# Attention scores by one full float32 product instead of three products of rounded halves, in a fused attention and feed-forward kernel

## Chip, cores and metric

The kernel runs on one core of a Trainium2 chip. The metric is device time in microseconds of one launch, as the median of several runs. Before the change it is 913.26 us, the median of three runs from 912.97 to 914.45 us.

## What is computed

Attention over 8 batches of 8 heads, with keys and values averaged over blocks of 8 tokens, followed by a feed-forward layer. Queries and keys are drawn 8 times larger than normal, so that the scores have to be accurate.

```python
# q, k, v: (8, 8, 576, 64) float32
k_p = k.reshape(B, H, 72, 8, D).mean(axis=3)
v_p = v.reshape(B, H, 72, 8, D).mean(axis=3)
scores = scale * np.matmul(q, k_p.transpose(0, 1, 3, 2))
scores = scores - np.max(scores, axis=-1, keepdims=True)
attn = np.exp(scores)
attn = attn / (np.sum(attn, axis=-1, keepdims=True) + 1e-09)
x = np.matmul(attn, v_p)        # to (4608 tokens, 512)
h = x @ w_in                    # 512 -> 2048
g = h * erf(softplus(h))
out = g @ w_out                 # 2048 -> 512
```

The scores alone are what the change touches.

## The kernel before

**Numbers in halves.** The products use the type `float32r`, into which values are rounded. What must be accurate is made of three such products: high half by high half, high by low, low by high. The high half is a rounded copy of a value (a cast on ACT, sometimes DVE or POOL), the low half is the difference (a subtraction on DVE or POOL).

**Chunks.** The 4608 tokens are worked off in nine chunks of 512. The first two chunks use plain products for the first layer (`gemm1`, L817). From the third on, a scheme with seven half-size products in place of eight does it (`products`, L762). The second layer (`gemm2`, L866) is the same for all.

**Attention.** `job` (L510) handles one block of up to 320 tokens of one batch. Keys of a new batch are summed over 8 tokens into `ks` and stored, as high and low halves, in `kbd`, a block-diagonal array: for each of the four pairs of heads, 144 columns of high halves and 144 of low ones, with the two heads of a pair on partitions 0 to 63 and 64 to 127. `softmax_tile` then takes up to 128 queries. There are 40 such tiles: 32 with 128 queries and 8 with 64. A tile's queries come by DMA into `raw`; ACT makes `qh` (L346, a helper for all copies; some go to DVE or POOL at L349 and L347), POOL or DVE makes `ql` (L584).

**Scores before.** In the first two chunks, and for tiles of 64 queries throughout, PE makes three products for each pair of heads (L618), 144 columns each: 12 a tile, in two groups of two pairs. DVE takes the maximum of a group from PSUM (L623) and, outside the first chunk, subtracts it (L640). In the first chunk ACT takes the exponential straight from PSUM with the maximum as its bias (L634). From the third chunk on a tile of 128 queries is scored in another form (25 tiles, `wide_scores`). For each pair of heads, the high half of the queries goes over all 288 columns of `kbd` (L594), and the low half over 144 (L596), which is two weight loads and two products in place of three and three. This form leaves two partial sums side by side, so ACT copies one out (L600), DVE adds the other (L602), takes the maximum of all eight heads (L605) and subtracts it (L607).

After that the tile's softmax (L649 to L666) is the same in both forms. PE transposes the result (L673, L680), and four products with the values for each pair of heads follow (L714).

**Order.** No engine's order is written by hand. The program is recorded as operations with an engine, a guessed cost and a due time, and `Program.order` lays them out greedily by these guesses; each engine then executes its own list strictly in order. Buffers have fixed numbers of copies: `raw` 2, `qh` and `ql` 1 each, PSUM 8 banks with caps by use. The first chunk borrows the space of late weights for a second `qh` and `ql` (`LENT_Q`). While PE has nothing to do in the first 57 us of the planner's time, the planner puts dummy products into its list (L929, 202 of them). DMA is issued by SP, in the same planned order.

Of the kernel before, what the change touches and what calls it, by code (L numbers as in the profile page):

```python
# [11 lines left out]
F32 = mybir.dt.float32  # L12
# [39 lines left out]
ON_ACT = ((1, 1), (1, 1), (1, 1), (1, 1))  # L52

LENT_E = ("wo15", "wo14", "wo13")
LENT_Q = ("wi15", "wo12")
LENT_KV = ("wo8", "wo9", "wo10", "wo11", "wi9", "wi10", "wi11", "wi12", "wi13", "wi14")
WIDE_FROM = 2
SLACK, BIAS = 34, 1150
FILL, MARGIN = 57000.0, 300
DGE = 2000  # L60
# [244 lines left out]
def moe_attention(ctx: ExitStack, tc: tile.TileContext, cst, qa, kl, vl, wi, wo, out):  # L305
# [3 lines left out]
    if wide:  # L309
# [2 lines left out]
    ctx.enter_context(tc.manual_schedule(engines={E.PE, E.Activation, E.DVE, E.Pool, E.SP}))  # L312

    const = pool("const", 1)
    sizes = {"t": 8, "raw": 2, "qh": 1, "ql": 1, "eth": 1, "etl": 1, "etb": 1,
             "s": 2, "m": 2, "z": 2, "bb": 1, "ks": 1, "vs": 1, "hs": 3, "y": 1, "f": 2, "gh": 3, "gl": 2}
    pools = {t: pool(t, n) for t, n in sizes.items()}
    banks = pool("banks", 8, space=PSUM)
# [14 lines left out]
    def dve(n):  # L333
        return 1.04 * n + 95
# [38 lines left out]
    def late(tag, shape, dtype=F32):  # L373
        return Buf(weights, [P] + shape, dtype, tag, [tag])

    kbd = const.tile([P, NP, 4 * SP], F32R, name="kbd")
    vah = const.tile([P, NP, P], F32R, name="vah")
    val = const.tile([P, NP, P], F32R, name="val")
    vb = const.tile([P, NP, D], F32R, name="vb")
    nc.gpsimd.memset(kbd.bitcast(F32), 0.0)  # L380
    KBD, VA, VB = (Kept() for _ in range(3))
    def f32(ap):
        return ap.bitcast(F32)
# [126 lines left out]
    def job(ck, b, tiles, off, times, first, fresh):  # L510

        base, due = times[0], times[-1] + VAL_R
        if fresh:
            ks, vs = buf("ks", [NP, SP]), buf("vs", [NP + 2, D])

            on_dve = b < ON_DVE

            def load_pool(src, dst, p, size, prio, tag):
                t = (loan if tag in LENT_KV else buf)(tag, [size, POOL] if on_dve else [POOL, size])
                op("SP", (14.4 if first and p < NP and size == SP else 10.3) * size, prio - 1, lambda: nc.sync.dma_start(  # L520
                    t.ap, src.rearrange("(p a b) -> p a b", p=P, b=t.ap.shape[2])), [], [t])
                if on_dve:
                    op("DVE", dve(8 * size), prio, lambda: nc.vector.tensor_reduce(
                        dst.ap[:, p, :], t.ap, AX.X, ALU.add), [t], [(dst, p)])
                else:
                    op("POOL", gps(4 * size), prio, lambda: nc.gpsimd.tensor_add(  # L526
                        t.ap[:, 0:4], t.ap[:, 0:4], t.ap[:, 4:8]), [t], [t])
                    op("POOL", gps(2 * size), prio, lambda: nc.gpsimd.tensor_add(  # L528
                        t.ap[:, 0:2], t.ap[:, 0:2], t.ap[:, 2:4]), [t], [t])
                    op("POOL", gps(size), prio, lambda: nc.gpsimd.tensor_add(  # L530
                        dst.ap[:, p, :], t.ap[:, 0], t.ap[:, 1]), [t], [(dst, p)])

            for p in range(NP):
                load_pool(kl[b, p], ks, p, SP, base + KEYS + KEYS_R * p,
                          "s" if first and p > 1 else LENT_KV[p] if b == 1 and wide else "raw")
            for r0, c0 in ((64, 0), (0, SP)):
                hi = kbd[r0:r0 + 64, :, c0:c0 + SP]
                lo = kbd[r0:r0 + 64, :, 2 * SP + c0:2 * SP + c0 + SP]
                sl = slice(r0, r0 + 64)
                op("ACT", act(4 * SP), base + KEYS_S, lambda hi=hi, sl=sl: nc.scalar.copy(hi, ks.ap[sl]),  # L540
                   [ks], [(KBD, (r0, 0))])
                both(b < 2, dve(4 * SP), gps(4 * SP), base + KEYS_S, lambda e, hi=hi, lo=lo, sl=sl: e.tensor_sub(
                    lo, ks.ap[sl], f32(hi)), [ks, (KBD, (r0, 0))], [(KBD, (r0, 1))])
            for p in range(NP + 2):
                load_pool(vl[b, p], vs, p, D, base + VALS + VALS_R * p,
                          ("gh" if p % 2 else "gl") if first else LENT_KV[NP + p] if b == 1 and wide else "raw")
            for i in range(2):
                mk = c[:, C_MA + i:C_MA + i + 1]
                sl = slice(D * i, D * i + D)
                op("ACT", act(4 * D) + 95, due + VALS_S, lambda mk=mk, sl=sl: nc.scalar.activation(  # L550
                    vah[:, :, sl], vs.ap[:, 0:NP, :], AF.Copy, scale=mk), [vs], [(VA, (0, i))])
                op("DVE", dve(4 * D) + 60, due + VALS_S, lambda mk=mk, sl=sl: nc.vector.scalar_tensor_tensor(
                    val[:, :, sl], vs.ap[:, 0:NP, :], mk, f32(vah[:, :, sl]), ALU.mult, ALU.subtract),
                   [vs, (VA, (0, i))], [(VA, (1, i))])
            vm = buf("f", [NP, D])
            both(b < 2, dve(4 * D), gps(4 * D), due + VALS_S, lambda e: e.tensor_mul(
                vm.ap.rearrange("r (g x) d -> r g x d", x=2),
                vs.ap[:, NP:].unsqueeze(2).broadcast_to([P, 2, 2, D]),
                c[:, C_MB:C_MB + NP].rearrange("r (g x) -> r g x", x=2).unsqueeze(3).broadcast_to([P, 2, 2, D])),
                 [vs], [vm])  # L560
            copy(b < 2, 4 * D, due + VALS_S, lambda: vb, lambda: vm.ap, [vm], [VB])
            both(b < 2, dve(4 * D), gps(4 * D), due + VALS_S, lambda e: e.tensor_sub(
                vb[64:96], vm.ap[64:96], f32(vb[64:96])), [vm, VB], [VB])
# [6 lines left out]

        def softmax_tile(at, qo, T, r):
            k, cs = at, slice(at, at + T)
            wide_scores = T == P and ck >= WIDE_FROM
            raw, qh, ql = (buf("hs" if ck == 0 else "raw", [NP, P]), *(
                loan(LENT_Q[i], [NP, P], F32R) if ck == 0 and off + at & P and wide else buf(t, [NP, P], F32R)
                for i, t in enumerate(("qh", "ql"))))
            s, m, z, bb = buf("s", [H, SP]), buf("m", [H]), buf("z", [H]), buf("bb", [NP, 16])
            op("SP", 5.2 * T + 400 * (first and at == 0), r - (Q_DUE if first else 2), lambda: nc.sync.dma_start(raw.ap[:, :, :T], 
                qa[qo:qo + P * NP * T].rearrange("(p n t) -> p n t", p=P, n=NP)),
               [], [raw])  # L580
            copy(ck < 2, 4 * T, r - 0.6, lambda: qh.ap[:, :, :T], lambda: raw.ap[:, :, :T], [raw], [qh])

            def low(e):
                return e.tensor_sub(ql.ap[:, :, :T], raw.ap[:, :, :T], f32(qh.ap[:, :, :T]))  # L584

            op("POOL", gps(4 * T), r - 0.5, lambda: low(nc.gpsimd), [raw, qh], [ql],
               alt=("DVE", dve(4 * T), lambda: low(nc.vector)) if first else None, port=True)
            if wide_scores:
                for p in range(NP):
                    ps = bank("att")  # L590
                    hs = slice(2 * p, 2 * p + 2)

                    def pair_scores(p=p, ps=ps):
                        nc.tensor.matmul(ps.ap[:T, :4 * SP], qh.ap[:, p, :T], kbd[:, p, :],  # L594
                                         start=True, stop=False, skip_group_check=True)
                        nc.tensor.matmul(ps.ap[:T, :2 * SP], ql.ap[:, p, :T], kbd[:, p, :2 * SP],  # L596
                                         start=False, stop=True, skip_group_check=True)

                    op("PE", 243, r + 0.05 * p, pair_scores, [qh, ql, KBD], [ps], [s, m, z])
                    op("ACT", act(2 * SP, True), r + 0.3, lambda ps=ps, hs=hs: nc.scalar.copy(  # L600
                        s.ap[:T, hs], ps.ap[:T, 2 * SP:4 * SP].rearrange("p (h k) -> p h k", k=SP)), [ps], [(s, p)])
                    op("DVE", dve(2 * SP), r + 0.4, lambda ps=ps, hs=hs: nc.vector.tensor_add(  # L602
                        s.ap[:T, hs], s.ap[:T, hs], ps.ap[:T, :2 * SP].rearrange("p (h k) -> p h k", k=SP)),
                       [ps, (s, p)], [(s, p)])
                op("DVE", dve(H * SP), r + 0.5, lambda: nc.vector.tensor_reduce(  # L605
                    m.ap[:T], s.ap[:T], AX.X, ALU.max), [s], [m])
                op("DVE", dve(H * SP), r + 0.6, lambda: nc.vector.tensor_sub(  # L607
                    s.ap[:T], s.ap[:T], m.ap[:T].unsqueeze(2).broadcast_to([T, H, SP])), [s, m], [s])
            for g in range(0 if wide_scores else 2):
                ps = bank("att")  # L610
                pv = lambda ps=ps: ps.ap[:T, :4 * SP].rearrange("p (h k) -> p h k", k=SP)

                def scores(ps=ps, g=g):
                    for pp in range(2):
                        p = 2 * g + pp
                        o = ps.ap[:T, 2 * SP * pp:2 * SP * pp + 2 * SP]
                        for i, (q, ko) in enumerate(((qh, 0), (qh, 1), (ql, 0))):
                            nc.tensor.matmul(o, q.ap[:, p, :T], kbd[:, p, 2 * SP * ko:2 * SP * ko + 2 * SP],  # L618
                                             start=(i == 0 and pp == 0), stop=(i == 2), skip_group_check=True)

                op("PE", 6 * 111, r, scores, [qh, ql, KBD], [ps], [s, m, z])
                gs = slice(4 * g, 4 * g + 4)
                op("DVE", dve(4 * SP), r + 0.4, lambda pv=pv, gs=gs: nc.vector.tensor_reduce(  # L623
                    m.ap[:T, gs], pv(), AX.X, ALU.max), [ps], [(m, g)])
# [349 lines left out]
```

## Time and profile before

| quantity | value |
|---|---|
| median of the runs | 913.26 us |
| span of the profiled execution (the page gives no time of its own for what lies around it) | 912.5 us |
| TensorE clock granted, mean | 0.997 |
| PE busy, instructions | 898 us, 5534 |
| weight loads (PEld) busy | 795 us |
| ACT busy | 678 us |
| DVE busy | 659 us |
| POOL busy | 362 us |
| DMA, mean | 193 GB/s |

The median of the runs is 0.8 us above the span. A product's duration in the trace runs from its start to the modelled end of its pipeline, and the durations of neighbours overlap. What a product costs PE is therefore read from the distance between starts: in the trace, twelve products of 256 columns last 283 ns each, yet start about 120 ns apart. Rows name what is written, then `<-`, then what is read; a row that ends in `[0.23 <-DVE ql L584]` had its engine idle for 0.23 us before it, until that instruction was done.

### The profile page before, as it was taken

What the parts mean: (1) busy time and instruction counts of PE and PEld (TensorE: products, weight loads), DVE (VectorE), ACT (ScalarE), POOL (GpSimd) and SP (SyncE); (2) the same over time, 40 slices, a digit from 0 to 9 for tenths busy, and PEclk for the clock granted to TensorE, in tenths of its full rate; (3) what the DMA queues carried; (4) which work ended last, traced back from release to release, by engine and by line L of the source; (5) the groups of instructions that cost most, each with busy time, mean ns of one, the idle gap of its engine ahead of it and who ended that gap; (6) DMA issues with size and microseconds to landing.
All of it is one profiled execution on the core that took longest, in us unless ns stands there. A gap on an engine that the chain in (4) does not pass through costs nothing.

```text
span 912.5 us, 15938 instructions
## 1 busy us (share of the span) xinstructions
PE 897.5 (98%) x5534; PEld 794.6 (87%) x5534; DVE 658.6 (72%) x1378; ACT 677.7 (74%) x1190; POOL 361.8 (40%) x473
## 2 busy tenths in 40 slices
PE   8899999999999999999999999999999999999998
PEld 7777878887898899999989999999989989999996
DVE  7888888898987875557778767776977666575332
ACT  4799896887877777766877777777778777676664
POOL 3689877335264433234354334352342211020110
PEclk9999999999999999999999999999999999999999
DMA  8994133444386566654675557565655564446521
GB/s 307 404 408 150 36 129 101 154 183 170 116 287 229 169 216 232 231 184 158 221 261 173 194 174 252 200 218 173 226 192 167 188 198 168 163 173 215 178 81 47
DMA packets 68256, 176.23 MB, mean 193 GB/s; under 512 B 11216, under 2 KB 13392, under 8 KB 68176
## 3 DMA queue, kind: packets, MB, share of 16 engines
q1 hardware_dynamic: 67888, 174.69, 55.6%
q8 instruction: 44, 0.72, 0.3%
q10 hardware_dynamic: 288, 0.52, 0.2%
q14 instruction: 36, 0.29, 0.1%
HBM read 151.06 MB, written 24.12 MB: 192 GB/s over the span
## 4 chain that ended last, share of the span: by engine, by line
PE 80%; DVE 3%; ACT 2%; POOL 2%; issue 1%; POOLq 0%; ACTq 0%
PE banks L866 39%; PE banks L762 30%; PE banks L817 4%; PE banks L714 3%; PE banks L594 1%; PE banks L673 1%; PE banks L596 1%; DVE hs L845 0%; PE banks L618 0%; PE banks L680 0%; DVE t L475 0%; DVE f L465 0%; ACT L835 0%; POOL raw L528 0%; POOL raw L526 0%
## 5 line engine op out<-in xcount | busy, mean ns | idle before, releaser
L866 PE MATMUL banks<-wo,gh 128*128 128x512 f32 x1152 | 363.8, 397 | 0.2 <-POOL wo L423 0.2
L762 PEld LDWEIGHTS banks<-t,wi 128*128 128x128 f32 x2352 | 303.0, 191 | 11.9
L762 PE MATMUL banks<-t,wi 128*128 128x256 f32 x2352 | 310.3, 283 | 0.0
L866 PEld LDWEIGHTS banks<-wo,gh 128*128 128x128 f32 x1152 | 202.4, 189 | 32.4 <-POOL wo L423 0.6
L866 PE MATMUL banks<-wo,gl 128*128 128x512 f32 x576 | 225.0, 391 | 0.0
L866 PEld LDWEIGHTS banks<-wo,gl 128*128 128x128 f32 x576 | 108.2, 188 | 24.2
L835 ACT ACT_TABLE_LOAD x72 | 92.4, 1283 | 33.4 <-DVE wi L780 18.1
L780 DVE TENSOR_TENSOR wi<-wi,banks 128x256 f32<-128x256 f32 x168 | 67.5, 415 | 45.7 <-PE banks L762 19.7
L817 PE MATMUL banks<-t,wi 128*128 128x512 f32 x384 | 94.9, 399 | 1.0 <-DVE y L845 0.9
L817 PEld LDWEIGHTS banks<-t,wi 128*128 128x128 f32 x384 | 72.0, 191 | 16.7 <-DVE y L845 1.4
L526 POOL TENSOR_TENSOR raw<-raw 128x256 f32<-128x256 f32 (+1 forms) x60 | 48.5, 809 | 75.3 <-DMA raw<-vl 24.5
L842 ACT ACTIVATE y<-y 128x1024 f32<-128x1024 f32 (+1 forms) x73 | 76.2, 1046 | 0.7
L584 POOL TENSOR_TENSOR ql<-raw,qh 128x512 fp32r<-128x512 f32 (+1 forms) x36 | 43.8, 1215 | 79.5 <-ACT qh L346 50.7
L842 ACT ACT_TABLE_LOAD x58 | 74.4, 1283 | 1.0
L847 ACT CAST gh<-hs 128x512 fp32r<-128x512 f32 x72 | 44.4, 620 | 29.6 <-PE banks L866 20.4
L852 POOL TENSOR_TENSOR gl<-hs,gh 128x512 fp32r<-128x512 f32 x24 | 32.5, 1353 | 77.1 <-PE banks L866 31.1
L852 DVE TENSOR_TENSOR gl<-hs,gh 128x512 fp32r<-128x512 f32 x48 | 34.4, 716 | 38.5 <-PE banks L866 36.0
L780 DVE TENSOR_TENSOR hs<-wi,banks 128x256 f32<-128x256 f32 x84 | 33.0, 417 | 33.4 <-PE banks L762 32.7
L847 ACT CAST gh<-wi 128x512 fp32r<-128x512 f32 x56 | 34.6, 619 | 25.7 <-PE banks L866 15.7
L845 DVE TENSOR_TENSOR hs<-y,hs 128x512 f32<-128x512 f32 x72 | 50.4, 730 | 4.4 <-ACT y L842 4.1
L852 DVE TENSOR_TENSOR gl<-wi,gh 128x512 fp32r<-128x512 f32 x38 | 27.1, 713 | 32.9 <-PE banks L866 32.4
L600 ACT COPY s<-banks 128x144 f32<-128x144 f32 x100 | 25.5, 280 | 26.0 <-PE banks L596 25.7
(162 smaller groups left out, 1491.3 us busy)
## 6 DMA issues: line engine op xcount, KB each, us to landing
wi<-w SPq DMA_DIRECT2D x168, 512.0 KB, 3.9
wi<-w SPq DMA_DIRECT2D x56, 256.0 KB, 4.5
raw<-vl SPq DMA_DIRECT2D x36, 256.0 KB, 3.5
wi<-wi SPq DMA_DIRECT2D x16, 512.0 KB, 9.2
wo<-wo SPq DMA_DIRECT2D x16, 512.0 KB, 9.6
w<-t SPq DMA_DIRECT2D x16, 512.0 KB, 3.4
raw<-kl SPq DMA_DIRECT2D x26, 288.0 KB, 3.1
raw<-qa SPq DMA_DIRECT2D x28, 256.0 KB, 4.5
```

The source lines that it names most:

```text
L526: op("POOL", gps(4 * size), prio, lambda: nc.gpsimd.tensor_add(t.ap[:, 0:4], t.ap[:, 0:4], t.ap[:, 4:8]), [t], [t])
L584: return e.tensor_sub(ql.ap[:, :, :T], raw.ap[:, :, :T], f32(qh.ap[:, :, :T]))
L714: nc.tensor.matmul(d, w, e, start=(i == 0), stop=(i == 3), skip_group_check=True)
L762: nc.tensor.matmul(dst(), weight(name, w, p), x[:, xl, p, :], start=(first and p == 0 and q == 0), stop=(p == 1 and q == 2), skip_group_ch ...
L780: return op("DVE", dve(HALF), prio, lambda: nc.vector.tensor_add(dst(), x(), b.ap[:, side]), reads + [b], writes)
L817: nc.tensor.matmul(ph.ap, w_in[ft].ap[:, w, P * p:P * p + P], xs[p].ap[:, x], start=(p == 0 and q == 0), stop=(p == NP - 1 and q == 2))
L835: nc.scalar.activation(y.ap[:, half(k)], hh[k].ap, AF.Softplus)
L842: op("ACT", act(w), n + 1.9, lambda sl=sl: nc.scalar.activation(y.ap[:, sl], y.ap[:, sl], AF.Erf), own, own, funcs="sigmoid")
L845: op("DVE", dve(TC), n + 1.9, lambda k=k: nc.vector.tensor_mul(g(k), y.ap[:, half(k)], hh[k].ap), [(y, k), hh[k]], [gs[k]], port=kept)
L847: op("ACT", act(TC), n + 2.0, lambda k=k: nc.scalar.copy(gh[k].ap, g(k)), [gs[k]], [gh[k]], port=True, alt=("DVE", 0.52 * TC + 150, lambda ...
L852: return e.tensor_sub(gl[k].ap, g(k), f32(gh[k].ap))
L866: nc.tensor.matmul(o[t].ap, g.ap[:, gs], w_out[ft].ap[:, w], start=(ft == 0 and q == 0), stop=(ft == NJ - 1 and q == 2))
```

## The change

The queries are no longer split. PE multiplies the loaded queries, as float32, with unsplit float32 keys: one product for each pair of heads, two in a group, four a tile, for all 40 tiles. So these go away: the copies into `qh`, the subtractions into `ql`, the low half of `kbd` and its subtractions, the wide form with its copies (L600), additions (L602), whole-tile maximum (L605) and subtraction (L607). The 25 wide tiles now take the maximum and subtract it by groups straight from PSUM, as the others did. `raw` gets four buffers in place of two. The planner books 300 ns a product (`SCORES`).

```diff
-LENT_Q = ("wi15", "wo12")
-WIDE_FROM = 2
+SCORES = 300
...
-    sizes = {"t": 8, "raw": 2, "qh": 1, "ql": 1, "eth": 1, "etl": 1, "etb": 1,
+    sizes = {"t": 8, "raw": 4, "eth": 1, "etl": 1, "etb": 1,
...
-    kbd = const.tile([P, NP, 4 * SP], F32R, name="kbd")
+    kbd = const.tile([P, NP, 2 * SP], F32, name="kbd")
...
-                op("ACT", act(4 * SP), base + KEYS_S, lambda hi=hi, sl=sl: nc.scalar.copy(hi, ks.ap[sl]),
-                   [ks], [(KBD, (r0, 0))])
-                both(b < 2, dve(4 * SP), gps(4 * SP), base + KEYS_S, lambda e, hi=hi, lo=lo, sl=sl: e.tensor_sub(
-                    lo, ks.ap[sl], f32(hi)), [ks, (KBD, (r0, 0))], [(KBD, (r0, 1))])
+                own = kbd[r0:r0 + 64, :, c0:c0 + SP]
+                op("ACT", act(4 * SP), base + KEYS_S, lambda own=own, r0=r0: nc.scalar.copy(own, ks.ap[r0:r0 + 64]),
+                   [ks], [(KBD, r0)])
...
-            copy(ck < 2, 4 * T, r - 0.6, lambda: qh.ap[:, :, :T], lambda: raw.ap[:, :, :T], [raw], [qh])
...
-            op("POOL", gps(4 * T), r - 0.5, lambda: low(nc.gpsimd), [raw, qh], [ql],
-               alt=("DVE", dve(4 * T), lambda: low(nc.vector)) if first else None, port=True)
-            if wide_scores:
...
-                        nc.tensor.matmul(ps.ap[:T, :4 * SP], qh.ap[:, p, :T], kbd[:, p, :],
-                                         start=True, stop=False, skip_group_check=True)
-                        nc.tensor.matmul(ps.ap[:T, :2 * SP], ql.ap[:, p, :T], kbd[:, p, :2 * SP],
-                                         start=False, stop=True, skip_group_check=True)
...
-            for g in range(0 if wide_scores else 2):
+            for g in range(2):
...
-                        for i, (q, ko) in enumerate(((qh, 0), (qh, 1), (ql, 0))):
-                            nc.tensor.matmul(o, q.ap[:, p, :T], kbd[:, p, 2 * SP * ko:2 * SP * ko + 2 * SP],
-                                             start=(i == 0 and pp == 0), stop=(i == 2), skip_group_check=True)
-
-                op("PE", 6 * 111, r, scores, [qh, ql, KBD], [ps], [s, m, z])
+                        nc.tensor.matmul(o, raw.ap[:, p, :T], kbd[:, p, :], start=(pp == 0), stop=True,
+                                         skip_group_check=True)
+
+                op("PE", 2 * SCORES, r, scores, [raw, KBD], [ps], [s, m, z])
```

Since the planner lays everything out anew, the order moves on all engines. Two places matter below.

The first is PE, late in the program, at the last tile that has 128 queries. `qh`, `ql` and `raw` are that tile's queries, `t` and `wi` the operands of the first layer, `gh`, `gl` and `wo` those of the second. Before:

```order
L762 MATMUL banks_9383<-t_8994,wi12_9239 128x256 x6
L594 MATMUL banks_9443<-kbd_125,qh_9204 128x288
L596 MATMUL banks_9443<-kbd_125,ql_9209 128x144
L594 MATMUL banks_9447<-kbd_125,qh_9204 128x288
L596 MATMUL banks_9447<-kbd_125,ql_9209 128x144
L594 MATMUL banks_9451<-kbd_125,qh_9204 128x288
L596 MATMUL banks_9451<-kbd_125,ql_9209 128x144
L866 MATMUL banks_9285<-wo2_1150,gh_9293 128x512 x2
```

After the change, at the same tile:

```order
L725 MATMUL banks_8785<-t_8379,wi9_8638 128x256 x6
L581 MATMUL banks_8837<-kbd_119,raw_7821 128x144 x2
L581 MATMUL banks_8842<-kbd_119,raw_7821 128x144 x2
L829 MATMUL banks_8723<-wo2_1053,gh_8736 128x512 x2
L829 MATMUL banks_8723<-wo2_1053,gl_8771 128x512
```

Four pairs of products in four PSUM banks (three of them in the rows above, one earlier) became two groups of two products in two banks. Among the same neighbours, PE now waits for `raw` itself and no longer for `qh` and `ql`.

The second is the head of DVE's list, before the first exponentials; `ks` are the summed keys, `vs` the summed values, `m` the maxima. Before:

```order
L523 TENSOR_REDUCE ks_168<-s_173 128x72
L349 CAST qh_184<-hs_176 128x512
L542 TENSOR_TENSOR kbd_125<-ks_168,kbd_125 64x4x72 x2
L584 TENSOR_TENSOR ql_193<-hs_176,qh_184 128x512
L584 TENSOR_TENSOR wo12_197<-hs_179,wi15_188 128x512
L523 TENSOR_REDUCE vs_261<-gl_190 128x64
L523 TENSOR_REDUCE vs_261<-gh_195 128x64
L523 TENSOR_REDUCE vs_261<-gl_199 128x64
L623 TENSOR_REDUCE m_294<-banks_254 128x4
```

After the change:

```order
L522 TENSOR_REDUCE ks_162<-s_167 128x72
L586 TENSOR_REDUCE m_229<-banks_221 128x4
L590 TENSOR_SCALAR m_229<-m_229 128x4
L522 TENSOR_REDUCE vs_237<-gl_179 128x64
L586 TENSOR_REDUCE m_229<-banks_224 128x4
L522 TENSOR_REDUCE vs_237<-gh_227 128x64
L522 TENSOR_REDUCE vs_237<-gl_234 128x64
L590 TENSOR_SCALAR m_229<-m_229 128x4
```

The five instructions of splitting have left DVE's head, and the first maximum follows the last sum of keys directly.

More of the change, by code (lines that the diff above doesn't have):

```diff
@@ L379, in moe_attention @@
     vb = const.tile([P, NP, D], F32R, name="vb")
-    nc.gpsimd.memset(kbd.bitcast(F32), 0.0)
+    nc.gpsimd.memset(kbd, 0.0)
     KBD, VA, VB = (Kept() for _ in range(3))
@@ L536, in job @@
             for r0, c0 in ((64, 0), (0, SP)):
[L537 to L540, printed above, removed]
-                   [ks], [(KBD, (r0, 0))])
-                both(b < 2, dve(4 * SP), gps(4 * SP), base + KEYS_S, lambda e, hi=hi, lo=lo, sl=sl: e.tensor_sub(
-                    lo, ks.ap[sl], f32(hi)), [ks, (KBD, (r0, 0))], [(KBD, (r0, 1))])
+                own = kbd[r0:r0 + 64, :, c0:c0 + SP]
+                op("ACT", act(4 * SP), base + KEYS_S, lambda own=own, r0=r0: nc.scalar.copy(own, ks.ap[r0:r0 + 64]),
+                   [ks], [(KBD, r0)])
             for p in range(NP + 2):
@@ L572, in softmax_tile @@
             k, cs = at, slice(at, at + T)
[L573 to L576, printed above, removed]
+            raw = buf("hs" if ck == 0 else "raw", [NP, P])
             s, m, z, bb = buf("s", [H, SP]), buf("m", [H]), buf("z", [H]), buf("bb", [NP, 16])
@@ L580, in softmax_tile @@
                [], [raw])
-            copy(ck < 2, 4 * T, r - 0.6, lambda: qh.ap[:, :, :T], lambda: raw.ap[:, :, :T], [raw], [qh])
-            def low(e):
-                return e.tensor_sub(ql.ap[:, :, :T], raw.ap[:, :, :T], f32(qh.ap[:, :, :T]))
-            op("POOL", gps(4 * T), r - 0.5, lambda: low(nc.gpsimd), [raw, qh], [ql],
-               alt=("DVE", dve(4 * T), lambda: low(nc.vector)) if first else None, port=True)
-            if wide_scores:
[L589 to L594, printed above, removed]
-                                         start=True, stop=False, skip_group_check=True)
-                        nc.tensor.matmul(ps.ap[:T, :2 * SP], ql.ap[:, p, :T], kbd[:, p, :2 * SP],
-                                         start=False, stop=True, skip_group_check=True)
[L599 to L608, printed above, removed]
-            for g in range(0 if wide_scores else 2):
+            for g in range(2):
                 ps = bank("att")
```

## The prediction

> **What bounds the kernel now.** I read the page first: busy shares, DMA by slices, the chain that ended last.
>
> ```profile
> span 912.5 us, 15938 instructions
> ...
> PE 897.5 (98%) x5534; PEld 794.6 (87%) x5534; DVE 658.6 (72%) x1378; ACT 677.7 (74%) x1190; POOL 361.8 (40%) x473
> ...
> DMA  8994133444386566654675557565655564446521
> ...
> PE 80%; DVE 3%; ACT 2%; POOL 2%; issue 1%; POOLq 0%; ACTq 0%
> ```
>
> PE is busy for 98% of the span, and the chain runs over PE for 80%. The other engines have a quarter of their time left, POOL more than half. Busy PE need not be full PE, so the waits of PE come next: who was waited for, us in total, times, longest.
>
> ```profile
> PE banks L680 <- POOL bb L662: 3.4, 5, 1.3
> PE banks L929 <- DMA cst<-cst: 2.6, 1, 2.6
> PE banks L618 <- POOL ql L584: 1.6, 1, 1.6
> ...
> PE banks L596 <- POOL ql L584: 0.7, 1, 0.7
> ```
>
> That view has ten rows and little behind these: no wait that a faster neighbour could end is worth more than 3.4 us. Hence the time is what PE's own list takes. Freed time on DVE, ACT and POOL buys almost nothing, and each product made longer or shorter counts in full, except in the start, where dummy products fill PE's gaps.
>
> **What the removed products cost.** A product costs PE the distance to the next start, and what it delays in those that follow. The timeline of PE (start, duration, line) shows a wide pair by itself between long products:
>
> ```profile
> 521.18 0.30 PE L594 MATMUL banks<-kbd,qh 128*128 128x288 f32 x1
> 521.31 0.23 PE L596 MATMUL banks<-kbd,ql 128*128 128x144 f32 x1
> 521.38 0.67 PE L866 MATMUL banks<-wo,gh 128*128 128x512 f32 x2
> 521.89 0.39 PE L866 MATMUL banks<-wo,gl 128*128 128x512 f32 x1
> 522.12 0.62 PE L866 MATMUL banks<-wo,gh 128*128 128x512 f32 x2
> 522.58 0.40 PE L866 MATMUL banks<-wo,gl 128*128 128x512 f32 x1
> ```
>
> The pair takes 521.38 - 521.18 = 0.20 us. The two L866 products right behind it take 0.51 (521.89 - 521.38), and the next such two 0.46: a tail of 0.05. So a lone pair costs 0.25. In a row of pairs:
>
> ```profile
> 761.98 0.34 PE L594 MATMUL banks<-kbd,qh 128*128 128x288 f32 x1
> 762.15 0.23 PE L596 MATMUL banks<-kbd,ql 128*128 128x144 f32 x1
> 762.22 0.34 PE L594 MATMUL banks<-kbd,qh 128*128 128x288 f32 x1
> 762.40 0.23 PE L596 MATMUL banks<-kbd,ql 128*128 128x144 f32 x1
> 762.47 0.67 PE L866 MATMUL banks<-wo,gh 128*128 128x512 f32 x2
> ```
>
> Here a pair takes (762.47 - 761.98) / 2 = 0.245. I take 0.25 for each: 25 wide tiles x 4 pairs x 0.25 = **25.0 us**. A tile of 64 queries has three products for each pair of heads:
>
> ```profile
> 769.94 0.29 PE L618 MATMUL banks<-kbd,qh 128*64 128x144 f32 x2
> ...
> 770.13 0.30 PE L618 MATMUL banks<-kbd,qh 128*64 128x144 f32 x2
> ...
> 770.33 0.67 PE L866 MATMUL banks<-wo,gh 128*128 128x512 f32 x2
> ```
>
> From 769.94 to 770.33 there are two such threes: 0.20 each, 0.067 a product. A tile costs 4 x 0.20 and a tail, 0.85. By the order of PE's list seven of the eight lie behind the filled start: **6.0 us**. With 128 queries:
>
> ```profile
> 42.13 0.39 PE L618 MATMUL banks<-kbd,qh 128*128 128x144 f32 x2
> ...
> 42.47 0.39 PE L618 MATMUL banks<-kbd,qh 128*128 128x144 f32 x2
> ```
>
> Three products take 0.34, so 0.113 each, though the same 144 columns took 0.067 above; only the weights are twice as wide. Loading 128 columns of weights thus sets 0.113. The one such tile behind the start costs 12 x 0.113 = **1.35**. In all 25.0 + 6.0 + 1.35 = 32.35 us are removed.
>
> **What the new products cost.** The same 33 tiles get 4 x 33 = 132 full float32 products. The trace has none, so I bound one. The built program holds two weight loads and two products on PE for each of them (5478 products in all; with one for each there would be 5318). Bound below: two loads at 0.113, all else beside them, 0.23. Bound above: two loads of 0.113 that hide behind nothing and two streams of 0.13 (below), 0.49. If each of the two streams both halves of the 144 columns of keys, it streams 288, and the row with 288 columns is L594: 0.13 to the next start when it is alone, 0.17 to 0.18 in a row of pairs. I take 0.14, near the first, because the new scores stand in twos or fours between long products as the lone pair does: **0.28 a product**. 132 x 0.28 = 37.0 us. The new list has 48 separate runs of scores behind the start; with a tail of 0.05 each that adds 2.4. So 39.4 - 32.35 = **+7.0 us** on PE.
>
> By the Trainium skill's page "FP8 and Floating Point Precision", section "TensorE Precision Notes", true FP32 takes four passes through the array, one for each combination of halves: a rule that speaks against this change, which saves three. With the gap of the page "TensorE: Matmul & The Clock Gate", section "Back-to-back issue gap" (N / 2.4 + 2.5 ns), a product would be an estimated 4 x 62.5 = 250 ns, and the sum +3.1 in place of +7.0. That gap is 216 ns for 512 columns, where the rows above show 0.23, so the measured streams are kept.
>
> **Waits that go.** PE no longer waits for `ql`: 1.6 + 0.7 = **-2.3 us**. The other waits I leave as they are; a new order has others of that size, either way.
>
> **What the other engines lose.** From the groups, with shapes kept apart (count, busy us, mean ns):
>
> ```profile
> L584 POOL TENSOR_TENSOR ql<-raw,qh 128x512 fp32r<-128x512 f32 x28 | 37.8, 1351 | 51.9 <-ACT qh L346 41.6 <-DVE s L602 5.4 <-ACT gh L847 1.8
> L602 DVE TENSOR_TENSOR s<-s,banks 128x144 f32<-128x144 f32 x100 | 26.5, 297 | 11.1 <-ACT s L600 11.0
> L600 ACT COPY s<-banks 128x144 f32<-128x144 f32 x100 | 25.5, 280 | 26.0 <-PE banks L596 25.7
> L607 DVE TENSOR_TENSOR s<-s,m 128x576 f32<-128x576 f32 x25 | 24.9, 997 | 0.5
> L605 DVE TENSOR_REDUCE m<-s 128x8 f32<-128x576 f32 x25 | 18.8, 750 | 0.6
> L346 ACT ACTIVATE qh<-raw 128x512 fp32r<-128x512 f32 x27 | 17.0, 629 | 3.4 <-PE banks L618 1.8 <-DMA raw<-qa 1.1 <-POOL s L666 0.5
> ```
>
> ACT loses 25.5 + 17.0 us, POOL 37.8, DVE 26.5 + 24.9 + 18.8 less the maxima and subtractions by groups. All of it lies beside PE, and I count it as nothing. If that cover were gone, it would be a gain of at most the ten rows of waits. The added wait: scores now stand directly behind the DMA of `raw`, and all of PE's list, both layers, is queued behind them. Before, ACT's `qh` waited for that DMA for 1.1 us in all (last row), and `raw` now has four buffers, so I cost it at 0, at most 1.1.
>
> **The start.** Here PE waits for others, and DVE's and ACT's lists count:
>
> ```profile
> 8.41 0.42 DVE L349 CAST qh<-hs 128x512 fp32r<-128x512 f32 x1
> 9.05 0.94 DVE L542 TENSOR_TENSOR kbd<-ks,kbd 64x288 fp32r<-64x288 f32 x2 [0.22 <-ACT kbd L540]
> 9.91 0.68 DVE L584 TENSOR_TENSOR ql<-hs,qh 128x512 fp32r<-128x512 f32 x1
> 10.52 0.68 DVE L584 TENSOR_TENSOR wo<-hs,wi 128x512 fp32r<-128x512 f32 x1
> ...
> 18.40 0.75 DVE L523 TENSOR_REDUCE ks<-wo 128x72 f32<-128x576 f32 x1 [0.60 <-DMA wo<-kl]
> ```
>
> ```profile
> 11.91 0.63 ACT L346 ACTIVATE qh<-hs 128x512 fp32r<-128x512 f32 x1 [1.90 <-PE banks L618]
> 13.84 0.63 ACT L346 ACTIVATE wi<-hs 128x512 fp32r<-128x512 f32 x1 [1.30 <-DMA hs<-qa]
> ```
>
> DVE sheds 2.7 us by 11.1 us, as the head of its list shows. But at 18.40 it waits for keys of the second batch, with DMA 80% busy in that slice, and the new list has the same sum of keys ahead of the first multiplication of exponentials. What is won before is waited for there. I take **0**, with a bound of -4.0 (2.7 on DVE and 1.3 on ACT, all in series) and +1.1 if the wait of ACT for `raw` comes to stand on PE.
>
> **Sum.** +7.0 - 2.3 + 0 = +4.7: a span of 912.5 + 4.7 = 917.2. The median of the runs is 0.8 above the span, which gives **918.0 us**.
>
> **Rivals.**
> - *Four passes at the pace of the narrow tiles, no tail.* At 0.067 a pass a product is 0.268, and PE's list +3.0; less 2.3 gives +0.7, 914.0 us, no change. For it: the row at 769.94. Against it: the tail behind every run of short products above. The two pages cited above give the same outcome, +3.1 - 2.3. Chance 0.19.
> - *Faster: the start comes forward.* If the list behind 18.40 does move up by the 4.0 us and a product costs 0.26 (two lone L594 rows), the sum is 34.3 + 2.4 - 32.35 - 2.3 - 4.0 = -2.0, 911.3 us. It decides only if a product is below some 0.262; above that it ends as no change. For it: DVE's head. Against it: the wait for DMA at 18.40. Chance 0.15.
> - *The loads don't hide.* With one load of 0.11 a product left open, 0.28 + 0.11 = 0.39, PE gets 14.5 more: 932.5 us. Against it: weight loads are 87% busy beside a PE that is 98% busy. Chance 0.13.
> - *The change is not one product.* In the built program it is two, as counted above; that is in the forecast.
>
> **How the numbers follow.** The forecast (915 to 925 us) has 0.53. A measurement of this kernel tells 0.2%, 1.8 us, from no change. So faster has 0.15, within 0.2% 0.19, slower 0.53 + 0.13 = 0.66. The lower bound of a product, 0.23, gives 30.4 + 2.4 - 32.35 - 2.3 = -1.9, 911.4 us, and with a little of the start the low end is 910. The upper, 0.49, would give 946; I stop at 930, where a product is 0.37, and leave most of the open-load case out.
>
> **What would show it.** In the changed profile: 320 products of `kbd` with `raw` or `hs`, about 0.14 us apart within a run; no wait of PE for `ql`; DVE some 30 us and POOL some 45 us less busy; PE's first L780 product near 43 us, as the L817 product before:
>
> ```profile
> 43.29 3.02 PE L817 MATMUL banks<-t,wi 128*128 128x512 f32 x12
> ```
>
> If the starts of scores lie 0.12 or less apart, or the first L780 comes at 40 us, I am wrong on the fast side. If a load stands open between them, or PE waits for a DMA of `raw`, I am wrong on the slow side.

## Result and profile after

| kernel | median, us | runs | lowest to highest |
|---|---|---|---|
| before | 913.12 | 4 | 911.88 to 914.45 |
| after | 920.68 | 4 | 920.08 to 921.47 |

The ratio is 1.0081, with an interval from 1.0069 to 1.0094: the change makes the kernel 7.6 us slower. The profiled execution has a span of 918.4 us, against 912.5. It took 920.17 us, so 1.8 us lie around its span, and the runs of before that were timed beside the experiments show 1.8 as well (medians 913.1 and 911.3). The traced execution of before was thus about 1.2 us longer than the median of its kernel, the 0.8 us read ahead of the prediction is 1.0 too small (the forecast is the median of before and 4.7 either way), and the spans show only 5.9 of the 7.6 us.

First the page of the kernel after the change, its span, busy shares and chain:

```profile
span 918.4 us, 15541 instructions
...
PE 902.2 (98%) x5478; PEld 793.3 (86%) x5478; DVE 621.3 (68%) x1309; ACT 643.3 (70%) x1063; POOL 296.9 (32%) x423
...
PE 83%; DVE 7%; DMA 4%; ACT 3%; issue 1%; POOL 1%; SPq 0%; DVEq 0%; ACTq 0%; POOLq 0%
```

DVE does 37 us less, ACT 34 and POOL 65. PE is busy for 98% as before, and only the time has grown. In the chain DVE stands for 7% where it had 3%: less work on DVE, yet more of the end hangs on it.

PE's waits from 43 us on, where few dummy products are left to fill them (us in total, times, longest):

```profile
PE banks L636 <- DVE s L603: 2.0, 1, 2.0
PE banks L643 <- POOL bb L625: 0.9, 2, 0.6
PE banks L780 <- DVE y L808: 0.8, 1, 0.8
PE banks L643 <- DVE f L416: 0.4, 1, 0.4
```

No `ql` is left, and none of the rows names a DMA of `raw`. But the view has 5.2 us in all, and that of before, for the same stretch, 4.9: the 2.3 us that went have been replaced.

The first product of the first layer, 43.29 us before:

```profile
42.12 1.64 PE L780 MATMUL banks<-t,wi 128*128 128x512 f32 x6
```

**One full product.** PE's timeline at a run of two float32 products with 128 queries (start, duration, line; the number after the x counts PE's own products, and there are two for each in the code):

```profile
60.71 0.65 PE L581 MATMUL banks<-kbd,raw 128*128 128x144 f32 x4
61.10 0.72 PE L829 MATMUL banks<-wo,gh 128*128 128x512 f32 x2
61.66 0.40 PE L829 MATMUL banks<-wo,gl 128*128 128x512 f32 x1
61.90 0.62 PE L829 MATMUL banks<-wo,gh 128*128 128x512 f32 x2
62.36 0.39 PE L829 MATMUL banks<-wo,gl 128*128 128x512 f32 x1
```

The run takes 61.10 - 60.71 = 0.39 us. The two L829 products behind it take 0.56, the next such two 0.46: a tail of 0.10. That is 0.49 for two, **0.245 a product** with its tail. Before, a pair cost 0.245 to 0.25 with its tail. Nothing is won or lost there.

**With 64 queries** it is another matter. Two tiles' runs:

```profile
303.87 0.27 PE L643 MATMUL banks<-cst,bb 128*64 128x128 f32 x1
304.07 0.70 PE L581 MATMUL banks<-kbd,raw 128*64 128x144 f32 x4
304.70 1.69 PE L725 MATMUL banks<-t,wi 128*128 128x256 f32 x12
306.23 0.60 PE L636 MATMUL banks<-cst,s 128*128 128x128 f32 x4
306.76 0.70 PE L581 MATMUL banks<-kbd,raw 128*64 128x144 f32 x4
307.39 0.73 PE L829 MATMUL banks<-wo,gh 128*128 128x512 f32 x2
```

The same two products take 0.63 (304.70 - 304.07, and 307.39 - 306.76) though they load half the weights. Before, two pairs of heads of such a tile took 0.39 in six products.

**Where the span grew.** In the trace I took for each PE product the distance to the next start and summed these by what the product belongs to, from the first product of the first layer on:

| us | before | after | difference |
|---|---|---|---|
| until the first product of the first layer | 43.29 | 42.12 | -1.2 |
| dummy products behind it (22, then 32) | 2.27 | 4.15 | +1.9 |
| scores | 36.13 | 34.18 | -1.95 |
| transposes (L636, L643; L673, L680 before) | 15.94 | 20.73 | +4.8 |
| products with the values | 32.67 | 32.34 | -0.3 |
| both layers | 777.9 | 780.6 | +2.7 |

The sum is +5.9, the growth of the span (4.3 us from the last product's start to the end, the same in both, are in no row). A wait counts with the product ahead of it, a tail with the product behind. So the scores' -1.95 holds the 2.3 us of `ql` that went. What the score products cost the layers is in +2.7, and the largest term stands with the transposes, which the change does not touch; 3.2 of their +4.8 us are waits.

Each of the two traces also has one stretch of 3.4 us in which the granted clock was about half (0.51): from 71.1 us before, from 84.7 us after. Products of the first layer with 512 columns start 0.427 us apart there and 0.227 behind it. That costs either trace some 1.7 us, so it is no part of the difference between these two.

### The profile page after: what moved, and what is told of

Read it like the earlier page. It is cut to its first block, busy times and chain, and to the rows that moved or that the text cites. A ratio compares the mean times of both kernels' runs of the same rounds, so it can differ in the third digit from the quotient of the medians.

```text
span 918.4 us, 15541 instructions
## 1 busy us (share of the span) xinstructions
PE 902.2 (98%) x5478; PEld 793.3 (86%) x5478; DVE 621.3 (68%) x1309; ACT 643.3 (70%) x1063; POOL 296.9 (32%) x423
## 4 chain that ended last, share of the span: by engine, by line
PE 83%; DVE 7%; DMA 4%; ACT 3%; issue 1%; POOL 1%; SPq 0%; DVEq 0%; ACTq 0%; POOLq 0%
PE banks L829 39%; PE banks L725 30%; PE banks L780 6%; PE banks L677 3%; PE banks L581 3%; DMA wi<-wi 2%; PE banks L636 1%; DMA out<-f 1%; DVE t L474 1%; PE banks L892 1%; DMA w<-t 1%; ACT L798 1%; DVE banks L406 1%; DVE m L586 1%; DMA raw<-kl 0%
## 5 line engine op out<-in xcount | busy, mean ns | idle before, releaser
L829 PE MATMUL banks<-wo,gh 128*128 128x512 f32 x1152 | 364.6, 398 | 0.0
L725 PEld LDWEIGHTS banks<-t,wi 128*128 128x128 f32 x2352 | 305.1, 191 | 14.9 <-DVE hs L743 0.6
L725 PE MATMUL banks<-t,wi 128*128 128x256 f32 x2352 | 313.5, 283 | 0.1
L829 PEld LDWEIGHTS banks<-wo,gh 128*128 128x128 f32 x1152 | 203.2, 189 | 33.7 <-issue 1.0
L829 PE MATMUL banks<-wo,gl 128*128 128x512 f32 x576 | 225.0, 391 | 0.2 <-DVE gl L815 0.2
L829 PEld LDWEIGHTS banks<-wo,gl 128*128 128x128 f32 x576 | 108.2, 188 | 25.0 <-DVE gl L815 0.7
L815 POOL TENSOR_TENSOR gl<-hs,gh 128x512 fp32r<-128x512 f32 x26 | 34.7, 1336 | 123.2 <-PE banks L829 54.2
L581 PE MATMUL banks<-kbd,raw 128*128 128x144 f32 (+1 forms) x288 | 44.9, 289 | 0.0
L612 ACT ACTIVATE s<-s,cst 128x576 f32<-128x576 f32 (+1 forms) x36 | 27.9, 776 | 23.6 <-DVE s L603 23.0
```

Of the source, the lines that this page charges most:

```text
L581: nc.tensor.matmul(o, raw.ap[:, p, :T], kbd[:, p, :], start=(pp == 0), stop=True, skip_group_check=True)
L612: op("ACT", act(4 * SP * len(left)) + 93, r + 0.8, lambda gs=gs: nc.scalar.activation(s.ap[:T, gs], s.ap[:T, gs], AF.Sigmoid, bias=bias[0] ...
L725: nc.tensor.matmul(dst(), weight(name, w, p), x[:, xl, p, :], start=(first and p == 0 and q == 0), stop=(p == 1 and q == 2), skip_group_ch ...
L815: return e.tensor_sub(gl[k].ap, g(k), f32(gh[k].ap))
L829: nc.tensor.matmul(o[t].ap, g.ap[:, gs], w_out[ft].ap[:, w], start=(ft == 0 and q == 0), stop=(ft == NJ - 1 and q == 2))
```

## Experiments

Each of them was timed beside runs of the kernel before on the same chip, whose medians were 912.9 to 913.1 us. Two causes were weighed: the products themselves (those of 64 queries above all), and the order that the planner makes of the rest.

**Wider weights for the narrow tiles.** The queries of the 64-query tiles are loaded twice, side by side, so that the product loads 128 columns of weights. The planner's costs and the order stay.

```diff
-                        o = ps.ap[:T, 2 * SP * pp:2 * SP * pp + 2 * SP]
-                        nc.tensor.matmul(o, raw.ap[:, p, :T], kbd[:, p, :], start=(pp == 0), stop=True,
+                        o = ps.ap[:, 2 * SP * pp:2 * SP * pp + 2 * SP]
+                        nc.tensor.matmul(o, raw.ap[:, p], kbd[:, p, :], start=(pp == 0), stop=True,
...
```

> The changed kernel, but the tiles of 64 queries are loaded twice side by side, so that their score products load 128 columns of weights; the order of all engines is unchanged. Theory A (narrow weights): in the changed trace a run of full float32 products with 64 columns costs about 0.34 us more than one with 128 (0.09 ahead of it, 0.05 in its first product, 0.19 at its end, 0.01 behind it), and 12 such runs lie behind the start, so the time falls by about 4.0 us, to about 916.7. Theory B (a full product is dear everywhere, as predicted: 0.28 and a tail): nothing changes, 920.7 within 0.5.

Measured: 918.57 us, ratio 1.0063 (1.0049 to 1.0077), 2.1 us below the change. The timeline at the same place:

```profile
303.69 0.27 PE L643 MATMUL banks<-cst,bb 128*64 128x128 f32 x1
303.80 0.66 PE L581 MATMUL banks<-kbd,raw 128*128 128x144 f32 x4
304.19 1.69 PE L725 MATMUL banks<-t,wi 128*128 128x256 f32 x12
305.72 0.60 PE L636 MATMUL banks<-cst,s 128*128 128x128 f32 x4
306.16 0.66 PE L581 MATMUL banks<-kbd,raw 128*128 128x144 f32 x4
306.56 0.71 PE L829 MATMUL banks<-wo,gh 128*128 128x512 f32 x2
```

The run takes 0.39 in place of 0.63, and the product ahead of it 0.11 in place of 0.20. From L643 to L725 it is 0.50 against 0.83, from L636 to L829 0.84 against 1.16: a run of float32 products with 64 columns of weights costs **0.33 us more** than one with 128. A dozen such runs lie behind the start, 4 us, of which 2.1 reach the time: the first product of the first layer came 0.7 us later here (42.85), and some is lost in waits. The wait of 2.0 us for L603 is there as before.

**The 128-query products twice.** Each is issued two times in a row, in the same order; the second overwrites the first with the same values.

```diff
-                    for pp in range(2):
+                    for pp in (0, 1) * (2 if T == P else 1):
```

> The changed kernel with every score product of the tiles of 128 queries issued twice in the same place (the second result replaces the first, same values); the planner isn't told, so the order is the same. It prices one product in its place. Theory A: 0.245 us each with nothing behind it: 26 tiles behind the start x 4 x 0.245 = +25.5, about 946.2. Theory B: 0.28 and more: +29 or above, 949.7 or more. If PE were not the bound, clearly less than +25.

Measured: 942.41 us, ratio 1.0321 (1.0307 to 1.0335), 21.7 us above the change for 104 products behind the start, 0.21 each. The waits of PE in this kernel, over the whole span, show where the rest of the 0.245 went:

```profile
PE banks L892 <- DMA cst<-cst: 2.6, 1, 2.6
PE banks L636 <- DVE s L603: 2.0, 1, 2.0
...
PE banks L643 <- POOL bb L625: 0.3, 1, 0.3
```

PE's wait for POOL's `bb` is 0.3, where it was 3.5 in the change: a longer PE list gives its neighbours time. All the waits of that view add up to 7.2 us, against 11.3 in the change. A product's cost on PE's list is thus not quite what it costs the kernel.

**The same work in other orders.** Only the planner's price of a score product is altered, 245 and 330 in place of 300.

```diff
-SCORES = 300
+SCORES = 245
```

> The changed kernel with the planner's cost of a score product set to 245 in place of 300: the same instructions in another order. Theory C (part of the loss is the order: waits of 2.0 and 0.8 us near 82 us that the old order didn't have): the time moves by 1 to 3 us, the wait near 82 us is gone or elsewhere, and the distances between score products stay at 0.122. Rival: it stays within 0.5 us of the changed kernel, since PE's sum is the same.

> The same with 330 in place of 300. Theory C: again 1 to 3 us from the changed kernel, up or down, and not the same as with 245. Rival: within 0.5 us of it.

Measured: 926.68 us (925.79 to 932.23), ratio 1.0162 (1.014 to 1.0185), with 245; 932.39 us (930.02 to 933.37), ratio 1.0209 (1.0194 to 1.0223), with 330. The nearly exact price, 245, makes the kernel 6 us slower, 330 makes it 12 us slower, both more than the 1 to 3 us expected. PE's waits with 245, then with 330:

```profile
PE banks L643 <- POOL bb L625: 3.9, 4, 1.5
PE banks L636 <- DVE y L808: 2.7, 2, 2.1
...
PE banks L677 <- DVE f L416: 2.1, 1, 2.1
PE banks L636 <- DVE s L629: 1.7, 2, 1.2
```

```profile
PE banks L636 <- DVE s L629: 3.4, 2, 1.8
PE banks L780 <- ACT f L848: 3.1, 1, 3.1
...
PE banks L643 <- DVE t L693: 2.6, 1, 2.6
```

Each order waits somewhere else, mostly for steps of the softmax and of the layers. The waits are not all of it: the granted clock was half for 10.2 us of the trace with 245 and for 13.6 us of that with 330, against 3.4 us in the change, an estimated 3.4 and 5.1 us of the 6 and 12. So the order of the same work, with the clock that the runs were granted, can be worth as much as the whole result.

**The new products in the old order.** The kernel before, with all its operations, prices and its order, but one full float32 product in place of each pair in the 25 wide tiles; then also in place of each three in the others. The products use the high halves alone, so the low halves take no part in the scores; ACT's copy is scaled by 0, so that DVE's addition adds nothing. The edit of the wide tiles:

```diff
-                        nc.tensor.matmul(ps.ap[:T, :4 * SP], qh.ap[:, p, :T], kbd[:, p, :],
-                                         start=True, stop=False, skip_group_check=True)
-                        nc.tensor.matmul(ps.ap[:T, :2 * SP], ql.ap[:, p, :T], kbd[:, p, :2 * SP],
-                                         start=False, stop=True, skip_group_check=True)
+                        nc.tensor.matmul(ps.ap[:T, :2 * SP], f32(qh.ap[:, p, :T]), f32(kbd[:, p, :2 * SP]),
+                                         start=True, stop=True, skip_group_check=True)
```

> The kernel before, its order on every engine unchanged, with one thing exchanged: in the 25 wide tiles PE makes one full float32 product of 144 columns for each pair of heads in place of the pair of products. It takes the rounded queries and keys as operands and leaves out their low halves; ACT and DVE do as many instructions as before (ACT's copy is scaled by 0). So the price of the product stands alone, without a new order. Theory A (0.122 + 0.122 us, no tail): 100 x (0.245 - 0.25) = -0.5 and up to 0.7 less wait for the low halves, 911.7 to 912.9. Theory B (0.28 and a tail): +5 less 0.7, 917.

> The same exchange in all 40 tiles; again the order of the kernel before, and again without the low halves. Against the run with wide tiles alone, theory A: a tile of 64 queries costs 8 x 0.122 + 0.34 = 1.32 in place of 0.85, or 1.66 where its two groups stand apart: +4.0 for seven tiles, -0.4 for a tile of 128, -1.6 for the wait for the low half: +2.0, 914 to 915. If all of the measured loss of 7.8 us were the price of products, this run would show it: about 920.7. Theory C (order) says that at least 4 us of the loss are missing here.

Measured: 914.18 us, ratio 1.0005 (0.9993 to 1.0018), with the wide tiles alone; 915.8 us, ratio 1.0029 (1.002 to 1.0039), with all. The timeline of the first, at the lone pair that the prediction read at 521.18:

```profile
521.40 0.41 PE L594 MATMUL banks<-kbd,qh 128*128 128x144 f32 x2
521.55 0.71 PE L864 MATMUL banks<-wo,gh 128*128 128x512 f32 x2
522.10 0.39 PE L864 MATMUL banks<-wo,gl 128*128 128x512 f32 x1
522.33 0.62 PE L864 MATMUL banks<-wo,gh 128*128 128x512 f32 x2
522.79 0.40 PE L864 MATMUL banks<-wo,gl 128*128 128x512 f32 x1
```

0.15 to the next start where the pair took 0.20, and a tail of 0.09 (0.55 against 0.46) where it left 0.05: 0.24 against 0.25. The wide tiles are neutral. With all tiles the products cost 2.7 us, of the 7.6. PE does not wait for `ql` in that kernel either, since no product reads it. It gains little by that: its waits from 43 us on are 4.6 us, against 4.9 before, and the longest is a new one, for a step that unpacks weights:

```profile
PE banks L814 <- ACT banks L398: 1.7, 1, 1.7
```

It ends at 68.70 us, ahead of the first layer's products; at that place the kernel before had waited 1.64 us for `ql`, until 69.44. The other **4.9 us** of the change come with what surrounds the products: the new order and the runs into which it groups them, the other form of the softmax, the four buffers of `raw`.

**How sensitive the old order is.** The kernel before, with the planner's price of a wide pair at 233 and 253 in place of 243.

```diff
-                    op("PE", 243, r + 0.05 * p, pair_scores, [qh, ql, KBD], [ps], [s, m, z])
+                    op("PE", 233, r + 0.05 * p, pair_scores, [qh, ql, KBD], [ps], [s, m, z])
```

> The kernel before with the planner's cost of a wide pair set to 233 in place of 243, nothing else: the same instructions in another order. Theory C (any new order of this program loses some us against the one before, which is a good one): 3 to 12 us slower, as the changed kernel's orders at 245 and 330 were against its order at 300. Rival (the order before is nothing special, and the loss after comes with the change): 912.9 within 1 us.

> The same with 253. Theory C: again 3 to 12 us slower, and another amount than with 233. Rival: 912.9 within 1 us.

Measured: 916.38 us, ratio 1.0032 (1.002 to 1.0044), and 914.29 us, ratio 1.001 (1.0001 to 1.0018). Both are slower than with 243, by 3.3 and 1.2 us, where 3 to 12 were expected of each: the order matters here too, by less than was thought.

**Narrow tiles with wide weights in the old order.** The kernel of 915.8 us, with the queries of 64-query tiles loaded twice as in the first experiment.

```diff
-                        nc.tensor.matmul(o, f32(qh.ap[:, p, :T]), f32(kbd[:, p, :2 * SP]),
+                        nc.tensor.matmul(o, f32(qh.ap[:, p]), f32(kbd[:, p, :2 * SP]),
...
```

> The order of before, one full product in all 40 tiles as in e6_swap_all (915.8 us), but the 64-query tiles load 128 weight columns (their queries come twice, side by side, and their copy into qh is twice as long). ql and its subtraction stay, unused by the products. Theory A (a run of products with 64 weight columns costs 0.34 us more; twelve of them or so stand behind the start, and nothing else separates e6 from e5): 1.5 to 3 us below e6, 913 to 914.3 us, level with before. Theory B (what e6 costs above e5 comes from elsewhere): no change against e6, 915.4 to 916.4 us.

Measured: 913.89 us, ratio 1.001 (1.0002 to 1.0018), 1.9 us below. Of the 2.7 us that the products cost in the old order, 1.9 are thus in the entry and exit of 64-column runs, of which this order has nine behind the start and not the twelve expected. Without these the full float32 product, with no wait for `ql`, stands within 0.1% of the kernel before.

**More orders, with wide weights.** The first experiment's kernel with the planner's price at 280, 310 and 320 in place of 300 (`SCORES` alone).

> The changed kernel with 64-query tiles padded (e1_pad, 918.6 us), laid out anew with the planner's price of a score product at 280 in place of 300: the same work in another order. Theory order (the same work spreads by some us with the order alone): anywhere from 914 to 926 us, differing from e1_pad by more than 1.4 us. Theory products (the loss is in the products): within 1 us of e1_pad, 917.6 to 919.6 us.

> As e10_pad280 with 310. Theory order: anywhere from 914 to 926 us, differing from e1_pad by more than 1.4 us. Theory products: 917.6 to 919.6 us.

> As e10_pad280 with 320. Theory order: anywhere from 914 to 926 us, differing from e1_pad by more than 1.4 us. Theory products: 917.6 to 919.6 us.

Measured: 924.84 us (923.27 to 929.11), ratio 1.0133 (1.0111 to 1.0154), with 280; 921.03 us, ratio 1.0088 (1.0073 to 1.0104), with 310; 921.32 us, ratio 1.0089 (1.0076 to 1.0102), with 320. With 300 it was 918.57. Identical work spreads over 6.3 us, and none of these orders reaches the kernel before. The slowest, 280, was traced at a granted clock of 1.00, so here it is not the clock that makes the order slow.

## Why the prediction was right, and where it was not

The time was 920.7 where 918.0 was forecast, within the range and on the side forecast. Its terms did worse than its sum, which came so near in part by luck: one was too large, and others that added time had been put at nothing.

**The new products** were put at 0.28 each and a tail of 0.05 a run. That is the term that was mis-sized. PE's own products lie 0.122 us apart in the trace, not 0.14, and the tail is 0.10. At 128 columns that gives 0.245 a product, tail included, against 0.25 for the pair removed: by the sum, 100 x 0.03 = 3.0 us before tails were to be lost on the wide tiles, and the experiment in the old order shows +1.1, with an interval that includes no change. The page "TensorE: Matmul & The Clock Gate" of the Trainium skill, section "Back-to-back issue gap", comes nearer: for 288 columns its formula, given there for a single product by itself, makes an estimated 122.5 ns, and the trace has 122. No run varies the columns, so the agreement may be chance. The prediction kept 0.14, because the 512-column products ran wider than that formula (0.23 against 216 ns); the L594 row it read, 0.13 alone, was nearer.

**The narrow tiles** were priced like the others. They hold most of what the products cost in the old order: 0.33 us more for each run, 1.9 to 2.1 us in the two experiments with wider weights. No row of before showed it, since its 64-query products were `float32r`, at 0.067 each.

With these prices 104 products with 128 columns cost 25.5 us, and 28 with 64 columns, in ten runs of two and two of four, 10.8: 36.3 in place of 39.4, or +3.9 on PE's list in place of +7.0. The scores and layers of the table, without their waits, grow by 3.9 as well. The rival of four passes, with 0.268 and no tail (+3.0), was nearer in this term; its 914.0 us did not come, because of the terms below.

Together the products were forecast at +7.0, and at +4.7 with the wait for `ql` gone. Measured in the old order, where that wait is gone as well, they cost +2.7.

**The waits.** The -2.3 us for `ql` is the other term that failed, together with the sentence "The other waits I leave as they are; a new order has others of that size, either way". Both waits for `ql` went, but the others grew from 2.6 to 5.2 us. Even in the old order the longer wait only gave way to one of 1.7 us for ACT at the same place. The new order has its costliest place near 80 us. Before, second-layer products stood here ahead of the transposes, without a wait:

```profile
80.49 0.61 PE L866 MATMUL banks<-wo,gh 128*128 128x512 f32 x2
80.95 0.39 PE L866 MATMUL banks<-wo,gl 128*128 128x512 f32 x1
81.18 0.60 PE L673 MATMUL banks<-cst,s 128*128 128x128 f32 x4
81.61 0.27 PE L680 MATMUL banks<-cst,bb 128*64 128x128 f32 x1
```

After the change, PE's timeline there is:

```profile
78.98 0.65 PE L581 MATMUL banks<-kbd,raw 128*128 128x144 f32 x4
80.07 0.27 PE L643 MATMUL banks<-cst,bb 128*64 128x128 f32 x1 [0.44 <-DVE f L416]
82.38 0.63 PE L636 MATMUL banks<-cst,s 128*128 128x128 f32 x4 [2.04 <-DVE s L603]
83.78 0.98 PE L780 MATMUL banks<-t,wi 128*128 128x512 f32 x3 [0.76 <-DVE y L808]
```

and DVE's, in the same stretch:

```profile
79.84 0.45 DVE L586 TENSOR_REDUCE m<-banks 128x4 f32<-128x288 f32 x1
80.21 1.23 DVE L629 TENSOR_TENSOR s<-s,z 128x576 f32<-128x576 f32 x1
81.47 0.28 DVE L650 TENSOR_TENSOR etb<-banks,etb 32x128 fp32r<-32x128 f32 x1
81.78 0.46 DVE L603 TENSOR_TENSOR s<-banks,m 128x288 f32<-128x288 f32 x1
```

PE stands idle for 0.44 + 2.04 + 0.76 = 3.2 us. Its list has transposes right behind one another, and the second ones (L636) need two things of DVE: the scaling of probabilities (L629), which DVE begins only at 80.21 and ends at 81.44, and their PSUM bank. In the built program it is the bank that holds the scores of 78.98, and the transposes wait until L603, the last reader of those scores, is done, at 82.24.

The last two of these waits are 2.8 us of the transposes' +4.8 in the table, and ten more dummy products behind the first layer's start make +1.9. Sorted by terms, without waits where not named, the +5.9 of the spans are +3.9 for the products, +0.3 for all waits, +1.6 for the transposes, +1.7 for the dummies, -0.3 with the values and -1.2 for the start.

Of the 4.9 us that the old order does not show, the two spans (914.0 and 918.4) show 4.4. By the same count of distances the transposes hold +4.15 of these, the dummies +1.4 and the scores +1.2, against -1.7 in the layers and -0.8 with the values. The sum of the waits hardly differs (4.6 and 5.2 us). Beside the dummies, the traces show two other differences: the stretch at half the granted clock, 1.7 us, which the trace in the old order does not have, and twelve runs with 64 columns in place of nine, an estimated 3 x 0.33 = 1.0 us. That the clock costs the kernel those 1.7 us is not shown: of the nine runs in the old order, those with a mean clock of 1.0 took 915.8 and 916.6 us, those with 0.998 from 914.9 to 918.3. That the order itself, and not the leaner softmax or the buffers, does it is not tested apart; that it can is shown by the six orders tried of the change's work, which lie between 918.6 and 932.4 us.

**The start** was put at 0, between -4.0 and +1.1; it came forward by 1.2 us. The rival in which it carries the result asked for a product below 0.262. The product is 0.245, tail included, and still that rival did not come: neither 4.0 us in the start nor 2.3 us of waits were kept.

**The other engines** lost 37 us (DVE), 34 (ACT) and 65 (POOL), more than was forecast for DVE and POOL and less than the 42.5 of ACT's two rows, and the time did not fall by it, as argued: PE's list did not get shorter.

**What would show it.** "0.12 or less apart" was to mean wrong on the fast side. The starts are 0.122 apart, and the time came out on the slow side of the forecast: this sign spoke of one term, and the terms that were set to nothing or taken off added more. PE waits for no DMA of `raw`, as forecast.

## What to carry to other kernels

Where one engine is busy for 98% and the order is laid out by a greedy planner, a change of the work is two changes, and the second, the new order, must be priced with a spread of its own: here 3 us for a move of 10 in one price (243 to 233), 6 us for one of 20 (300 to 280). The new operation in the old order (with results scaled away where they would disturb) separates the two. And count the instructions that run on the engine and their distance to the next start at every width in use: the float32 product was neutral with 128 columns of weights and dear with 64.

## Unexpected on the hardware

- A float32 product of 144 columns runs on PE as two products, each loading its own weights, 0.122 us apart with 128 weight columns, and it lengthens what follows by 0.10 us once a run, whether the run has two or four products.
- With 64 columns of weights the spacing within a run is the same 0.122, but the product ahead is held for 0.09 us more and the run takes 0.24 more (0.63 against 0.39). `float32r` products of the same shape, at 0.067 each, showed nothing of the kind. Why is open: only the width was varied, and widening it removes the whole cost.
- The granted clock was half from 84.7 to 88.1 us in the trace of the change, soon after PE's 3.2 us of waits, and from 71.1 to 74.5 us before, soon after the wait of 1.6 us for `ql`. Products of 512 columns started 0.427 us apart there. The traces with 233 and 253 have the same wait for `ql` and no such stretch, so what brings it about is open.
